# One float32r split for both heads of a pair, and two magnitude buffers, in a fused attention and expert kernel

## The chip, the cores and the metric

The kernel runs on one core of a Trainium2 chip. The metric is the device time of one execution in microseconds, taken as the median of three runs. A profiled execution of the same program gives the rows below.

## The reference, cut to what matters

```python
# q, k, v: (4 batches, 8 heads, 576 positions, 64 per head), float32
scores = (q @ k.T) / 8 + bias              # bias: -slope(head) * |i - j|
attn = softmax(where(0 <= i - j < 128, scores, -1e9))
x = (attn @ v).transpose(0, 2, 1, 3).reshape(2304, 512)
h = x @ w_in                               # (2304, 2048)
g = (a0 + a1*h + a2*h^2 + a3*h^3) / (1 + |b0|*|h| + |b1|*h^2 + 1e-6)
x = g @ w_out                              # w_in, w_out arrive as float64
e = argmax(x @ w_gate); p = softmax(x @ w_gate)[e]
out = p * (relu(x @ w1[e]) @ w2[e])        # 8 experts, 512 -> 1024 -> 512
```

## The kernel before, in words

The 2304 tokens are cut into nine chunks of 256 (`c` from 0 to 8). For each chunk there is an attention step over four pairs of heads (`hp`), which leaves `x` as two float32r halves `xh` and `xl`, and a first feed-forward step over eight pairs of weights (`j` from 0 to 7): `up` makes `h_ps`, `rational` makes `gh` and `gl` from it, and `down` adds to `y_ps` two steps later. While chunk `c` is in its feed-forward step, the attention of chunk `c + 1` runs beside it. Behind the ninth chunk the tokens are sorted by expert and ten chunks of expert work follow, with `load_split` fetching the expert weights.

Float32 accuracy on TensorE comes from splits. A tensor `a` becomes `hi = round(a)` in float32r and `lo = a - hi`, and products are made with both. For q and k of chunks 2 to 8 (`c >= PACK`) the kernel loads q and k of two heads so that each head lies twice over the 128 partitions: 64 rows for the high half and 64 for the low half. For each head `r` of the pair, it then takes one tile `qk` of the pool `rawp` and cuts it into `q2`, `kh` and `kl`. ScalarE (ACT) copies q into `q2` (L279) and k into `kh` (L280), VectorE (DVE) overwrites the lower half of `q2` with the remainder (L281), and GpSimd (POOL) makes `kl` (L284). TensorE (PE) makes the scores of one head by two matmuls (L307), one with `kh`, one with `kl`. Seven chunks of four pairs make 28 pairs, so each of these four lines stands 56 times in the program.

The first 16 weights arrive as float64 and are converted on the chip during chunk 0 (`convert`): `fetch64`, then `magnitude64` (ACT takes the absolute value, L174; DVE clamps it, L175), then `split64` (DVE L186, L189, L192; ACT L195; POOL L196). Weights 0 to 13 use tiles of the pool `ring`. Weights 14 and 15 come in halves: their raw halves share the two buffers of `rawp` with the `qk` tiles, and their magnitudes share the three buffers of the pool `ahp` with `ah` of `rational`. In the expert stage `load_split` takes `ah` and `u` buffers too, for every third weight (L212; its ACT copy is L215, its remainder L216).

`rational` uses `ah` (L387, freed by POOL at L392) and `u`, `qq`, `r0` from the pool `ep`, two buffers each. `u` is written by ACT (L388), worked on by DVE (L395, L396, L399, L405), copied by ACT (L408) and freed by POOL (L409, `gl`). The tiles of one name go round their buffers in the order of the program text, so a new tile waits until the one that had the buffer is freed.

The order on each engine is not written out by hand: the program is recorded, and a scheduler puts the instructions of the five queues in order before launch. Each engine then works its queue strictly in that order.

Of the kernel before, what the change touches and what calls it, by code (L numbers as in the profile page):

```python
# [11 lines left out]
F32 = mybir.dt.float32  # L12
F32R = mybir.dt.float32r
# [4 lines left out]
ALU = mybir.AluOpType  # L18
# [4 lines left out]
P = 128  # L23
T = 256
# [5 lines left out]
PACK = 2  # L30
# [11 lines left out]
def attention_rational_moe_kernel(  # L42
# [11 lines left out]
    nc = tc.nc  # L54
    B, _, S = qT.shape
    H, D, W = 8, 64, 128
    NT, DM = out.shape
# [8 lines left out]
    NSTAT = NCH  # L66

    const = ctx.enter_context(tc.tile_pool(name="const", bufs=1))
    ahp = ctx.enter_context(tc.tile_pool(name="ahp", bufs=3))
    xp = ctx.enter_context(tc.tile_pool(name="xp", bufs=2))  # L70
    rawp = ctx.enter_context(tc.tile_pool(name="rawp", bufs=RAWB))
    ring = ctx.enter_context(tc.tile_pool(name="ring", bufs=RING))
    ep = ctx.enter_context(tc.tile_pool(name="ep", bufs=2))
    ap_ = ctx.enter_context(tc.tile_pool(name="ap", bufs=2))
# [32 lines left out]
        out=upper, in_=ones, pattern=[[1, P]], compare_op=ALU.is_gt, fill=0.0,  # L107
# [11 lines left out]
    for h in range(H):  # L119
        sl = 2.0 ** (-8.0 * (h + 1) / H)  # L120
        nc.vector.tensor_scalar(
            out=bm[:, h, :], in0=rel, scalar1=-sl * D ** 0.5, scalar2=None, op0=ALU.mult
        )
        nc.gpsimd.affine_select(
            out=bm[:, h, :], in_=bm[:, h, :], pattern=[[-1, 2 * W]], compare_op=ALU.is_ge,
# [27 lines left out]
    mags = {}  # L153
# [14 lines left out]
    def magnitude64(f):  # L168
        if f < EARLY:
            mags[f] = [ring.tile([P, 2 * DM], F32, name="mag", tag="ring")]  # L170
        else:
            mags[f] = [ahp.tile([P, DM], F32, name="mag", tag="ah") for _ in range(2)]
        for raw, a in zip(raws[f], mags[f]):
            nc.scalar.activation(out=a, in_=raw.bitcast(F32)[:, :, 1], func=AF.Abs)  # L174
            nc.vector.tensor_scalar(  # L175
                out=a, in0=a, scalar1=F64_LEAST, scalar2=F64_MOST, op0=ALU.max, op1=ALU.min
            )
# [87 lines left out]
    def attention(c, xh, xl):  # L265
        for hp in range(H // 2):
# [5 lines left out]
            tiles, kc = load_qkv(c, hp, q_sb, k_sb, v_sb)  # L272


            qks = []
            for r in range(2 if c >= PACK else 0):
                qk = rawp.tile([P, 2 * DM], F32R, name="qk", tag="raw")
                q2, kh, kl = qk[:, 0:T], qk[:, T:T + kc], qk[:, 2 * T + W:2 * T + W + kc]
                nc.scalar.copy(q2, q_sb[:, r, :])  # L279
                nc.scalar.copy(kh, k_sb[:, r, 0:kc])  # L280
                nc.vector.tensor_tensor(  # L281
                    out=q2[D:P], in0=q_sb[D:P, r, :], in1=q2[D:P].bitcast(F32), op=ALU.subtract
                )
                nc.gpsimd.tensor_tensor(  # L284
                    out=kl, in0=k_sb[:, r, 0:kc], in1=kh.bitcast(F32), op=ALU.subtract
                )
                qks.append((q2, kh, kl))
            x_ps = ps_x.tile([P, T], F32, name="x_ps")
            for L, qcol, k0, wn, bo, blocks in tiles:
                s_ps = [ps_s.tile([P, 2 * W], F32, name="s_ps") for _ in range(2)]  # L290
# [5 lines left out]
                for r in range(2):  # L296
                    if c < PACK:
                        nc.tensor.matmul(
                            s_ps[r][0:L, 0:wn],
                            q_sb[D * r:D * r + D, qcol:qcol + L],  # L300
                            k_sb[D * r:D * r + D, k0:k0 + wn],
                            start=True, stop=True,
                        )
                        continue
                    q2, kh, kl = qks[r]
                    for i, kk in enumerate((kh, kl)):
                        nc.tensor.matmul(  # L307
                            s_ps[r][0:L, 0:wn], q2[:, qcol:qcol + L], kk[:, k0:k0 + wn],
                            start=(i == 0), stop=(i == 1),
                        )  # L310
                for r in range(2):
# [447 lines left out]
```

## Time and profile before

| | |
|---|---|
| median of three runs | 933.65 us (932.35 to 934.86) |
| the profiled execution, its own time | 939.27 us |
| its span, first to last instruction | 937.5 us |
| busy in the span: PE, DVE, ACT, POOL | 846.0, 729.0, 610.9, 486.5 us |
| mean granted TensorE clock | 0.962 of full speed |

The span is what the rows below show; some 1.8 us lie around it. A busy time is a sum over the whole span, and the stages differ: chunk 0 with its conversion, chunks 1 to 8, the sorting, and the experts. A granted clock under 1 means that TensorE ran a part of that stretch at the lower of its two levels, 1.2 GHz instead of 2.4 GHz.

### The profile page before, as it was taken

The page shows a single profiled execution, that of the slowest core. Times are in us where ns is not written, and L with a number is a line of the kernel's source. Part 1 is how long each engine was busy: PE and PEld are TensorE (multiplying, and loading weights), DVE is VectorE, ACT ScalarE, POOL GpSimd, SP SyncE. Part 2 cuts the span into 40 slices and gives each one's busy share as a digit, 9 for nine tenths or more (in the row PEclk, how much of TensorE's full clock was granted, in tenths as well). Part 3 has the DMA queues.
Part 4 walks back from the last instruction along what each step waited for, and adds up shares of the span by engine and source line. Part 5 has one row for each costly group of instructions (what it writes and reads, how often), then busy time and mean ns, then how long its engine had stood idle before and what let it go on. Part 6 is the DMA issues. An engine that isn't in the chain of part 4 may idle for free. (4 is left out here: it accounts for less than half of the span.)

```text
span 937.5 us, 16318 instructions
## 1 busy us (share of the span) xinstructions
PE 846.0 (90%) x5550; PEld 727.4 (78%) x5550; DVE 729.0 (78%) x1428; ACT 610.9 (65%) x1286; POOL 486.5 (52%) x403
## 2 busy tenths in 40 slices
PE   4547789998999899999999999999889999999994
PEld 2325568886888788878878878888778999999993
DVE  7999999797897998898987978869756985555510
ACT  5566658776887687778778768766636755555510
POOL 5444446553564555545645455535547875555500
PEclk9997989999999899999999999999988999999997
DMA  8554021123123222122122221100448976668300
GB/s 317 208 171 135 9 82 38 60 61 87 36 62 96 36 67 68 38 67 67 30 66 64 63 71 33 38 23 3 129 134 309 321 264 225 225 225 266 128 6 19
DMA packets 69959, 101.88 MB, mean 109 GB/s; under 512 B 14705, under 2 KB 47345, under 8 KB 68082
## 3 DMA queue, kind: packets, MB, share of 16 engines
q1 hardware_dynamic: 64658, 86.11, 28.9%
q0 software_dynamic: 5216, 14.70, 4.4%
q8 instruction: 45, 0.74, 0.3%
q14 instruction: 40, 0.33, 0.1%
HBM read 91.13 MB, written 10.17 MB: 108 GB/s over the span
## 5 line engine op out<-in xcount | busy, mean ns | idle before, releaser
L366 PE MATMUL h_ps<-x,w 128*128 128x256 f32 x896 | 261.3, 294 | 14.3 <-ACT w L195 5.2
L367 PE MATMUL h_ps<-x,w 128*128 128x256 f32 x896 | 261.5, 292 | 1.6 <-DVE x L354 1.2
L368 PE MATMUL h_ps<-x,w 128*128 128x256 f32 x896 | 260.8, 291 | 2.4 <-POOL w L196 1.6
L366 PEld LDWEIGHTS h_ps<-x,w 128*128 128x128 f32 x896 | 175.5, 197 | 24.4 <-ACT w L195 6.2
L375 PE MATMUL y_ps<-w,gh 128*128 128x512 f32 x448 | 182.4, 407 | 0.6 <-ACT gh L653 0.3
L367 PEld LDWEIGHTS h_ps<-x,w 128*128 128x128 f32 x896 | 176.5, 197 | 8.1 <-DVE x L354 2.3
L368 PEld LDWEIGHTS h_ps<-x,w 128*128 128x128 f32 x896 | 176.4, 197 | 6.7 <-POOL w L196 2.6
L376 PE MATMUL y_ps<-w,gh 128*128 128x512 f32 x448 | 179.6, 401 | 0.0
L377 PE MATMUL y_ps<-w,gl 128*128 128x512 f32 x448 | 170.7, 402 | 0.1
L409 POOL TENSOR_TENSOR gl<-u,gh 128x512 fp32r<-128x512 f32 x72 | 102.0, 1417 | 104.1 <-ACT gh L408 79.2
L392 POOL TENSOR_TENSOR qq<-qq,ah 128x512 f32<-128x512 f32 x72 | 101.2, 1405 | 96.1 <-ACT qq L389 93.0
L216 POOL TENSOR_TENSOR w<-rawh,w 128x512 fp32r<-128x512 f32 x60 | 86.7, 1467 | 52.8 <-ACT w L215 51.9
L377 PEld LDWEIGHTS y_ps<-w,gl 128*128 128x128 f32 x448 | 86.0, 192 | 19.0 <-issue 1.2
L317 ACT ACTIVATE p_sb<-p_sb,nm 128x256 f32<-128x256 f32 (+4 forms) x160 | 75.0, 470 | 38.3 <-DVE nm L312 37.8
L375 PEld LDWEIGHTS y_ps<-w,gh 128*128 128x128 f32 x448 | 86.4, 193 | 15.8 <-issue 1.5
L376 PEld LDWEIGHTS y_ps<-w,gh 128*128 128x128 f32 x448 | 86.5, 193 | 14.4 <-issue 0.2
L284 POOL TENSOR_TENSOR qk<-k_sb,qk 128x384 fp32r<-128x384 f32 (+1 forms) x56 | 65.5, 1180 | 38.0 <-ACT qk L280 30.7
L399 DVE SCALAR_TENSOR_TENSOR u<-u,co,r 128x512 f32<-128x512 f32 x72 | 64.8, 901 | 13.3 <-ACT r L394 12.8
L196 POOL TENSOR_TENSOR w<-mag,w 128x1024 fp32r<-128x1024 f32 (+1 forms) x18 | 44.8, 2489 | 51.6 <-ACT w L195 51.6
L395 DVE TENSOR_TENSOR u<-u,h_ps 128x512 f32<-128x512 f32 x72 | 48.9, 679 | 28.5 <-ACT u L388 28.3
L408 ACT CAST gh<-u 128x512 fp32r<-128x512 f32 x72 | 44.5, 618 | 38.6 <-DVE u L405 38.5
L216 DVE TENSOR_TENSOR w<-raw,w 128x1024 fp32r<-128x1024 f32 x30 | 49.4, 1646 | 25.7 <-ACT w L215 25.6
(140 smaller groups left out, 1673.9 us busy)
## 6 DMA issues: line engine op xcount, KB each, us to landing
rawh<-epack SPq DMA_DIRECT2D x100, 256.0 KB, 4.9
raw<-epack SPq DMA_DIRECT2D x30, 512.0 KB, 5.6
raw<-wpack SPq DMA_DIRECT2D x14, 1024.0 KB, 6.9
v_sb<-vv SPq DMA_DIRECT2D x92, 64.0 KB, 2.1
k_sb<-kT SPq DMA_DIRECT2D x28, 192.0 KB, 3.4
q_sb<-qT SPq DMA_DIRECT2D x40, 128.0 KB, 2.7
yd<-y_sb POOLq DMA_DIRECT2D x18, 256.0 KB, 2.6
k_sb<-kT SPq DMA_DIRECT2D x16, 160.0 KB, 3.0
```

The source lines that it names most:

```text
L216: (nc.gpsimd if i in POOLLO else nc.vector).tensor_tensor(out=w[:, 1, cs], in0=raw, in1=w[:, 0, cs].bitcast(F32), op=ALU.subtract)
L284: nc.gpsimd.tensor_tensor(out=kl, in0=k_sb[:, r, 0:kc], in1=kh.bitcast(F32), op=ALU.subtract)
L317: nc.scalar.activation(out=p_sb[0:L, r, 0:wn], in_=p_sb[0:L, r, 0:wn], func=AF.Exp, scale=-1.0, bias=nm[0:L, r:r + 1], accum_out=su[0:L, r ...
L366: nc.tensor.matmul(out_ps, w[:, 0, ws], xh[:, k, :], start=(k == 0), stop=False)
L367: nc.tensor.matmul(out_ps, w[:, 0, ws], xl[:, k, :], start=False, stop=False)
L368: nc.tensor.matmul(out_ps, w[:, 1, ws], xh[:, k, :], start=False, stop=(k == KD - 1))
L375: nc.tensor.matmul(y_ps[t], gh[:, i, ts], w[:, 0, DM:], start=a, stop=False)
L376: nc.tensor.matmul(y_ps[t], gh[:, i, ts], w[:, 1, DM:], start=False, stop=False)
L377: nc.tensor.matmul(y_ps[t], gl[:, i, ts], w[:, 0, DM:], start=False, stop=z)
L392: nc.gpsimd.tensor_tensor(out=qq, in0=qq, in1=ah, op=ALU.mult)
L399: nc.vector.scalar_tensor_tensor(out=u, in0=u, scalar=co[:, 0:1], in1=r0, op0=ALU.add, op1=ALU.mult)
L409: nc.gpsimd.tensor_tensor(out=gl, in0=u, in1=gh.bitcast(F32), op=ALU.subtract)
```

## The change

Both heads of a pair are split by one instruction per engine: `q2` is a tile of its own (a single buffer of 2 KB per partition in the pool of the attention), and `kh` and `kl` of both heads each take one of the two buffers of `rawp`. To pay for `q2`, the pool `ahp` goes from three buffers to two, and the magnitudes of weights 14 and 15 take one `ah` and one `u` buffer instead of two `ah`. The matmuls and their number stay the same.

```diff
-    ahp = ctx.enter_context(tc.tile_pool(name="ahp", bufs=3))
+    ahp = ctx.enter_context(tc.tile_pool(name="ahp", bufs=2))
...
-            mags[f] = [ahp.tile([P, DM], F32, name="mag", tag="ah") for _ in range(2)]
+            mags[f] = [
+                pool.tile([P, DM], F32, name="mag", tag=tag) for pool, tag in ((ahp, "ah"), (ep, "u"))
+            ]
...
-            qks = []
-            for r in range(2 if c >= PACK else 0):
-                qk = rawp.tile([P, 2 * DM], F32R, name="qk", tag="raw")
-                q2, kh, kl = qk[:, 0:T], qk[:, T:T + kc], qk[:, 2 * T + W:2 * T + W + kc]
-                nc.scalar.copy(q2, q_sb[:, r, :])
-                nc.scalar.copy(kh, k_sb[:, r, 0:kc])
+            if c >= PACK:
+                q2 = ap_.tile([P, 2, T], F32R, name="q2", bufs=1)
+                kh, kl = (
+                    rawp.tile([P, 2 * DM], F32R, name=name, tag="raw")[:, 0:2 * kc]
+                    .rearrange("p (r k) -> p r k", r=2) for name in ("kh", "kl")
+                )
+                nc.scalar.copy(q2, q_sb)
+                nc.scalar.copy(kh, k_sb[:, :, 0:kc])
                 nc.vector.tensor_tensor(
-                    out=q2[D:P], in0=q_sb[D:P, r, :], in1=q2[D:P].bitcast(F32), op=ALU.subtract
+                    out=q2[D:P], in0=q_sb[D:P], in1=q2[D:P].bitcast(F32), op=ALU.subtract
                 )
                 nc.gpsimd.tensor_tensor(
-                    out=kl, in0=k_sb[:, r, 0:kc], in1=kh.bitcast(F32), op=ALU.subtract
+                    out=kl, in0=k_sb[:, :, 0:kc], in1=kh.bitcast(F32), op=ALU.subtract
                 )
-                qks.append((q2, kh, kl))
...
-                    q2, kh, kl = qks[r]
                     for i, kk in enumerate((kh, kl)):
                         nc.tensor.matmul(
-                            s_ps[r][0:L, 0:wn], q2[:, qcol:qcol + L], kk[:, k0:k0 + wn],
+                            s_ps[r][0:L, 0:wn], q2[:, r, qcol:qcol + L], kk[:, r, k0:k0 + wn],
```

The scheduler makes a new order of it from the conversion of weight 14 on. Two places matter below. The first is POOL's queue at the end of chunk 0. Here `mag_1071` is the second half of weight 15, `qk_1397` and `qk_1402` (before) or `kl_1399` (of the change) belong to the first pair of chunk 2, and `u_990`, `u_1135`, `u_1191` to `rational` for `j` = 4, 5, 6. POOL's rows before:

```order
L284 TENSOR_TENSOR qk_1397<-k_sb_1383,qk_1397 128x384
L409 TENSOR_TENSOR gl_995<-u_990,gh_994 128x512
L392 TENSOR_TENSOR qq_1193<-qq_1193,ah_1192 128x512
L196 TENSOR_TENSOR w_1087<-mag_1071,w_1087 128x512
L284 TENSOR_TENSOR qk_1402<-k_sb_1383,qk_1402 128x384
L409 TENSOR_TENSOR gl_1140<-u_1135,gh_1139 128x512
```

POOL's rows of the change, at the same place:

```order
L411 TENSOR_TENSOR gl_995<-u_990,gh_994 128x512
L394 TENSOR_TENSOR qq_1193<-qq_1193,ah_1192 128x512
L288 TENSOR_TENSOR kl_1399<-k_sb_1383,kh_1398 128x768
L198 TENSOR_TENSOR w_1087<-mag_1071,w_1087 128x512
L411 TENSOR_TENSOR gl_1140<-u_1135,gh_1139 128x512
```

The two remainders of 384 columns, one on either side of the last half weight, have become one of 768 columns ahead of it.

The second place is DVE's queue just before that. `u_905` and `u_990` are those of `j` = 3 and 4, `mag_942` is the second half of weight 14, `mag_1070` the first of weight 15. DVE's rows before:

```order
L192 SCALAR_TENSOR_TENSOR mag_942<-raw64_925,mag_942 128x512
L322 RECIPROCAL ri_1221<-ri_1221 128x2
L312 ISA p_sb_1244,nm_1245<-s_ps_1242,bm_110 128x256
L312 ISA nm_1245 128x1
L312 ISA p_sb_1244,nm_1245<-s_ps_1243,bm_110 128x256
L312 ISA nm_1245 128x1
L175 TENSOR_SCALAR mag_1070<-mag_1070 128x512
L399 SCALAR_TENSOR_TENSOR u_905<-u_905,co_102,r0_908 128x512
L327 TENSOR_TENSOR p_sb_1219<-p_sb_1219,ri_1221 128x512
L354 TENSOR_TENSOR x_513<-x_ps_1017,x_513 128x256
L186 TENSOR_SCALAR mag_1070<-mag_1070 128x512
L405 SCALAR_TENSOR_TENSOR u_905<-qq_907,u_905 128x512
```

DVE's rows of the change from the end of `u_905` on:

```order
L407 SCALAR_TENSOR_TENSOR u_905<-qq_907,u_905 128x512
L323 TENSOR_REDUCE ri_1246<-sum0_188 128x2
L188 TENSOR_SCALAR mag_942<-mag_942 128x512
L324 RECIPROCAL ri_1246<-ri_1246 128x2
L177 TENSOR_SCALAR mag_1070<-mag_1070 128x512
L191 SCALAR_TENSOR_TENSOR mag_942<-raw64_925,mag_942 128x512
L329 TENSOR_TENSOR p_sb_1244<-p_sb_1244,ri_1246 128x512
L404 SCALAR_TENSOR_TENSOR qq_992<-qq_992,qc_106,r0_993 128x512
L188 TENSOR_SCALAR mag_1070<-mag_1070 128x512
L194 SCALAR_TENSOR_TENSOR mag_942<-raw64_925,mag_942 128x512
L285 TENSOR_TENSOR q2_1397<-q_sb_1382,q2_1397 64x512
```

Before, the second half of weight 14 was finished ahead of the end of `u_905`, and weight 15 had begun; in the change four of its DVE steps come behind it. In the rows that follow these in the change stand the steps of `u_990`.

## Rows read from the trace of the kernel before

**Rows 1.** Busy time by stretch of the span, engine by engine, with the granted clock.

```profile
core 0: us, PE busy (x) PEld busy (x) DVE busy (x) ACT busy (x) POOL busy (x), PEclk, DMA share, GB/s
98.00:156.00 58.00, 46.68 (x267) 38.10 (x268) 57.67 (x93) 36.72 (x74) 32.08 (x21) 0.88 0.18 50
156.00:610.00 454.00, 438.41 (x3096) 378.87 (x3095) 390.04 (x915) 348.07 (x818) 238.72 (x192) 0.98 0.21 58
610.00:720.00 110.00, 100.09 (x612) 87.05 (x611) 75.96 (x137) 62.50 (x107) 55.07 (x45) 0.92 0.33 111
720.00:937.00 217.00, 204.65 (x1322) 186.11 (x1320) 112.56 (x118) 102.33 (x165) 113.53 (x83) 0.98 0.56 190
```

**Rows 2.** PE's waits from 156 to 610 us: total us, times, longest.

```profile
PE pt_ps L336 <- DVE p_sb L327: 6.4, 6, 3.2
PE h_ps L366 <- ACT x L353: 1.9, 2, 1.1
PE s_ps L307 <- DVE qk L281: 1.4, 2, 0.8
```

**Rows 3.** L281 and L284 by source line: ns minimum/median/maximum.

```profile
L281 DVE TENSOR_TENSOR qk<-q_sb,qk x56: 416/476/2756, 139.4 to 601.5; 64x256 fp32r<-64x256 f32 x56
...
L284 POOL TENSOR_TENSOR qk<-k_sb,qk x56: 858/1166/2496, 136.2 to 600.4; 128x384 fp32r<-128x384 f32 x48, 128x320 fp32r<-128x320 f32 x8
```

**Rows 4.** Groups by shape, whole span: busy us, mean ns, idle before.

```profile
L281 DVE TENSOR_TENSOR qk<-q_sb,qk 64x256 fp32r<-64x256 f32 x56 | 41.3, 742 | 3.3 <-ACT qk L279 1.8
L327 DVE TENSOR_TENSOR p_sb<-p_sb,ri 128x512 f32<-128x512 f32 x44 | 40.7, 925 | 0.9
...
L284 POOL TENSOR_TENSOR qk<-k_sb,qk 128x384 fp32r<-128x384 f32 x48 | 58.0, 1218 | 26.9 <-ACT qk L280 20.9 <-PE y_ps L377 2.0 <-PE s_ps L307 1.6
L409 POOL TENSOR_TENSOR gl<-u,gh 128x512 fp32r<-128x512 f32 x72 | 102.0, 1417 | 104.1 <-ACT gh L408 79.2 <-issue 24.0 <-POOL qq L392 0.7
L196 POOL TENSOR_TENSOR w<-mag,w 128x1024 fp32r<-128x1024 f32 x14 | 38.6, 2757 | 49.3 <-ACT w L195 49.3
...
L279 ACT CAST qk<-q_sb 128x256 fp32r<-128x256 f32 x56 | 22.4, 402 | 7.0 <-PE s_ps L307 6.5 <-DMA q_sb<-qT 0.4
L280 ACT CAST qk<-k_sb 128x384 fp32r<-128x384 f32 x48 | 24.4, 511 | 1.2 <-DMA k_sb<-kT 1.2
L408 ACT CAST gh<-u 128x512 fp32r<-128x512 f32 x72 | 44.5, 618 | 38.6 <-DVE u L405 38.5
L195 ACT CAST w<-mag 128x1024 fp32r<-128x1024 f32 x14 | 14.6, 1044 | 17.5 <-DVE mag L192 17.2 <-DVE ri L322 0.3
```

**Rows 5.** Timeline of DVE, then of POOL, near 97 us: start, us.

```profile
96.90 2.84 DVE L175 TENSOR_SCALAR mag<-mag 128x1024 f32<-128x1024 f32 x1
...
100.32 0.68 DVE L186 TENSOR_SCALAR mag<-mag 128x1024 int32<-128x1024 int32 x1
...
96.41 2.78 POOL L196 TENSOR_TENSOR w<-mag,w 128x1024 fp32r<-128x1024 f32 x1 [5.58 <-ACT w L195]
```

**Rows 6.** L399 and L396 by source line: ns minimum/median/maximum.

```profile
L399 DVE SCALAR_TENSOR_TENSOR u<-u,co,r x72: 730/748/1792, 95.6 to 672.5; 128x512 f32<-128x512 f32 x72
...
L396 DVE SCALAR_TENSOR_TENSOR u<-u,co,h_ps x72: 720/746/749, 86.9 to 670.5; 128x512 f32<-128x512 f32 x72
```

**Rows 7.** Timeline at the end of chunk 0: `u` written, `gl` made.

```profile
124.66 0.77 ACT L388 ACTIVATE u<-h_ps,co 128x512 f32<-128x512 f32 x1
...
122.75 1.28 POOL L409 TENSOR_TENSOR gl<-u,gh 128x512 fp32r<-128x512 f32 x1 [3.60 <-ACT gh L408]
129.74 1.63 POOL L409 TENSOR_TENSOR gl<-u,gh 128x512 fp32r<-128x512 f32 x1 [2.60 <-issue]
```

**Rows 8.** As the experts begin: timelines of POOL and ACT; DMA issues, KB, us to landing.

```profile
663.75 1.45 POOL L392 TENSOR_TENSOR qq<-qq,ah 128x512 f32<-128x512 f32 x1 [2.12 <-ACT qq L389]
...
670.43 0.63 ACT L215 CAST w<-rawh 128x512 fp32r<-128x512 f32 x1
...
rawh<-epack SPq DMA_DIRECT2D x100, 256.0 KB, 4.9
```

## The prediction

> **What bounds the kernel now.** I read the busy times by stretch first, then what TensorE (PE) waits for in the stretch that the change touches most, and then the price of the split's instructions by shape. The cuts between the stretches are mine: chunk 0's conversion of weights ends near 156 us, attention ends near 610 us, the experts are under way by 720 us.
>
> From 156 to 610 us PE is busy 438.41 of 454 us, and its granted clock is 0.98 [rows 1]. So PE sets the time there. What another engine can give back is the 15.6 us in which PE is idle, and at most 0.02 x 454 = 9 us of clock. DVE comes next with 390 us, ACT has 348 and POOL 239. Of the 28 pairs all but the first are split there: 27 pairs, 54 of the 56 calls of each line. PE's largest named wait is for the normalized probabilities of DVE (L327), 6.4 us in 6 waits; it waits 1.4 us for the split of q (L281) and 1.9 us for `x` [rows 2]. The first is a wait for DVE's queue, the second for the work that is changed.
>
> From 98 to 156 us it is otherwise: DVE is busy 57.67 of 58 us, PE 46.68 [rows 1]. DVE sets the time there, and the magnitudes of weights 14 and 15 are part of its load. Behind 720 us PE is busy 204.65 of 217 us, and no instruction that the change rewrites runs there.
>
> **The change part by part.** PE's work is the same: the same matmuls on operands of the same shape. 0 us.
>
> *The split of q, DVE part (L281).* Two operations of 64x256 become one of 64x512. The trace has none of that shape; the nearest are the 128x512 operations with two operands in SBUF. By means, two cost 2 x 0.742 us and one of 512 columns 0.925 (L327) [rows 4], so a pair saves 0.56 us, and 27 pairs 15 us. By minima, two cost 2 x 0.416 [rows 3] and one 0.730 (L399) [rows 6]: 0.10 us per pair, 2.8 us in all. The means hold waits behind POOL, and one operation waits once where two wait twice; but not each pair waits. I take the middle, 9 us of DVE's 390.
>
> *The split of k, POOL part (L284).* Two operations of 384 columns cost 2 x 1.218 us. One of 768 lies between 1.417 (512 columns, L409) and 2.757 (1024 columns, L196) [rows 4]; halfway is 2.09. That saves 0.35 us per pair, 9 us over 27 pairs. The ends are a saving of 1.02 and a loss of 0.32 us per pair, 28 us and -9 us. I take halfway, since 768 is halfway in columns.
>
> *The copies on ACT.* For q, 2 x 0.402 becomes 0.618 (512 columns, L408); for k, 2 x 0.511 becomes 0.83, halfway between 0.618 and 1.044 (L195) [rows 4]. That is 0.19 us each and 10 us over 27 pairs. ACT is busy 348 of 454 us, so nearly all of this lies beside PE. If that cover were gone, the 10 us would be the price.
>
> *A longer hold of POOL against DVE.* Near 97 us a DVE step of 1024 columns took 2.84 us beside a POOL operation that ran from 96.41 to 99.19 us; another of that size took 0.68 beside none [rows 5]. L399 reads two operands in SBUF and reaches 1.792 us, while L396, which reads PSUM, never exceeds 0.749 [rows 6]. So DVE steps of some kinds wait until a POOL operation has ended. The change makes the longest hold in attention 0.87 us longer (2.09 against 1.218) while the sum of the holds falls by 9 us. PE waited for a step of that kind (L327) in only 6 places of the stretch [rows 2], so 6 x 0.87 = 5 us bounds the loss when each of these is hit in full. I take no loss, since the sum falls.
>
> The Trainium skill (SBUF — State Buffer, the section that sets engine ports apart from DMA ports) says that VectorE and GpSimd hold a shared pair of ports as an exclusive lock for a whole instruction, and that the other is blocked fully. The trace agrees with its 2.84 us against 0.68. By that rule alone a merged instruction is a longer block, which speaks against this change; by the rows the sum of the blocks falls.
>
> *The later start of head 0.* Head 0's scores need the `kl` of both heads now, 0.87 us later than before; head 1's come 0.35 us earlier. PE waited only 1.4 us for such work, and has `up` and `down` matmuls queued in between. 0 us, at most 28 x 0.87 = 24 us if every pair stood on PE's path; the row puts it far nearer to nothing.
>
> *Two `ah` buffers.* `ah` lives from ACT's L387 to POOL's L392, and `u` of the same step, with two buffers before and after, lives longer, to L409. So `u` binds first in the chunks: 0 us. In the expert stage `load_split` loads the half weight in `ah` one step later: it waits for the L392 of 663.75 to 665.20 us. A landing takes 4.9 us, so it is there at 670.1, and its ACT copy ran at 670.43 [rows 8]. The half in `u` is queued behind it on SP and waits for `gl`, as before. 0 us, at most 1.
>
> *The magnitude in `u`.* This is the dear part. The magnitudes of weights 14 and 15 now take turns with `u` of `rational`: `u` of `j` = 4 takes the buffer of `j` = 3, not that of `j` = 2. Before, it was written at 124.66 us, 0.6 us behind the `gl` that freed its buffer, which ended at 124.03. The `gl` of `j` = 3 ended at 131.37 [rows 7], so the bound of this wait is 6.7 us. But the order of DVE in the change ends `u_905` (`j` = 3) ahead of four conversion steps of weight 14, and puts them, with steps of weight 15, between it and `u_990`. Conversion and arithmetic of 512 columns cost 0.7 to 1.8 us a step [rows 6], so four steps bring that `gl` forward by 3 to 7 us and fill DVE meanwhile. DVE has to do the same work to the end of this stretch. 0 us, bounds -1 and +6.7. In POOL's queue the remainder of 768 columns stands ahead of the last half weight, which delays that by 2.09 - 1.22 = 0.9 us at most; it is the half that `down` uses, two steps later.
>
> **The sum.** DVE gets about 9 us lighter and is held off for some 9 us less from 156 to 610 us. PE's 15.6 us of idle time do not vanish with that, because most of it is the order of the queues and not load. I take a fifth, 3.1 us, and 0.4 us of clock. That fifth is a choice: of the 15.6 us, 7.8 are waits for L327 and L281, and I let two fifths of these go. All else is 0. The profiled execution took 939.27 us, 1.8 of it around the span: 939.27 - 3.5 = 935.8. It stands 5.6 us above the median of the runs, so the median comes to 933.65 - 3.5 = 930.2 us.
>
> **The rivals.** About 0.3% (2.8 us) is what a measurement of this kernel can tell from no change.
>
> *Hidden: no change.* The relief lands in DVE's, ACT's and POOL's own idle time. For it: PE is busy 97% and each of the three has at least 64 us of slack. Against it: half of PE's idle time is named as waits for DVE. Time 933 us, within 931 to 936. Chance 0.32.
>
> *A larger gain.* If the waits for DVE and the lower clock both go, PE gets 7.8 us and some 3 us of clock. For it: DVE by means is 15 us lighter. Against it: a new order makes new waits. Time 923 us. Chance 0.12.
>
> *Slower by the magnitude in `u`.* Place: 120 to 156 us. If the scheduler's order does not fill the wait, `u` of `j` = 4 to 6 each starts late. It decides from the point at which the chain from `gl` to the next `gl` outlasts the conversion steps between. For it: DVE has 0.3 us of slack there, and PE at a clock of 0.88 has little work that is ready. Against it: the order shown. Price 6.7 us: 940 us. Chance 0.14.
>
> *Slower by the longer hold.* Five to six us if the six waits for L327 grow by 0.87 and no relief reaches PE: 939 us. Against it stands the falling sum. Chance 0.09. The rule of the skill named above is the one that would bring it.
>
> My own forecast has 0.33, and its own range is 927 to 932.
>
> **How the numbers follow.** Faster than 930.85 us: the forecast's 0.33 and the larger gain's 0.12, so 0.45. Same: 0.32. Slower than 936.45: 0.14 + 0.09 = 0.23. The range reaches from the larger gain, 923, to the magnitude's price, 940, and leaves out a tenth on either side, where several waits come together.
>
> **What would show it.** In the profile after: PE's busy time within 1% of before, 28 operations less on DVE, 28 on POOL and 56 on ACT. The merged DVE step between 0.73 and 0.93 us, POOL's near 2.1, the q copy 0.62, the k copy 0.83. PE idle from the conversion's end to the end of attention near 12 us, with less wait for L327 and the q split. The stretch of chunk 0's end neither longer nor shorter by over 2 us; if it is longer, a wait of DVE or ACT for `gl` in 120 to 150 us stands in its place. The expert stage the same to 1 us. The prediction is wrong if PE's waits sit in new places, as the whole order is new, or if POOL's merged step costs nearer 2.7 us than 2.1.

## The result and the profile after

The change is slower: 945.46 us (median of 4 runs, 944.90 to 946.40) against 933.37 us for the kernel before (4 runs), a ratio of 1.0129 with a 95% interval of 1.0112 to 1.0147. Forecast were 930.2 us and a range of 923 to 940; the time lies 5.5 us above the range. The profiled execution took 945.52 us, at its median, with a span of 943.8 us. That of the kernel before stood 5.9 us above its median, so the two traces show only half of the 12 us between them: 6.3 us of span. These are 8.3 us more in which PE is idle and 2.0 us less in which it is busy (844.0 us, before 846.0), at a mean granted clock of 0.973 (before 0.962).

In the changed file the q copy is L283, the k copy L284, DVE's remainder of q L285 and POOL's remainder of k L288; lines behind them stand two higher than before. Busy time by stretch of the kernel after, which answers to [rows 1]:

```profile
core 0: us, PE busy (x) PEld busy (x) DVE busy (x) ACT busy (x) POOL busy (x), PEclk, DMA share, GB/s
98.00:156.00 58.00, 46.87 (x280) 37.94 (x281) 57.20 (x97) 38.78 (x77) 31.84 (x20) 0.91 0.18 52
156.00:610.00 454.00, 434.45 (x3066) 376.42 (x3066) 384.20 (x871) 334.30 (x749) 226.62 (x162) 0.98 0.21 57
610.00:720.00 110.00, 95.28 (x582) 81.80 (x579) 73.37 (x144) 61.73 (x108) 54.84 (x44) 0.95 0.27 94
```

From 156 to 610 us DVE, ACT and POOL are lighter, as intended, by 6, 14 and 12 us. PE is idle for 454 - 434.45 = 19.6 us instead of 15.6, and runs 30 matmuls fewer in that stretch. From 610 to 720 us it is idle for 14.7 us instead of 9.9. What PE waits for from 156 to 610 us in the kernel after (total us, times, longest), beside [rows 2]:

```profile
PE s_ps L309 <- DVE q L285: 7.5, 3, 4.8
PE h_ps L368 <- DVE u L398: 4.1, 7, 1.0
PE y_ps L377 <- ACT gh L410: 1.7, 2, 1.5
```

The waits for the normalized probabilities, 6.4 us before, are gone from the top. In their place stand the merged remainder of q, 7.5 us in three waits where its two parts cost 1.4 us, and `u`, for which the kernel before has

```profile
PE h_ps L366 <- DVE u L396: 1.2, 3, 0.5
```

The merged remainders by source line of the kernel after (ns minimum/median/maximum), beside [rows 3]:

```profile
L285 DVE TENSOR_TENSOR q<-q_sb,q x28: 689/1562/4374, 130.1 to 600.1; 64x512 fp32r<-64x512 f32 x28
...
L288 POOL TENSOR_TENSOR kl<-k_sb,kh x28: 1540/1849/2630, 142.7 to 600.5; 128x768 fp32r<-128x768 f32 x24, 128x640 fp32r<-128x640 f32 x4
```

The four merged operations as groups by shape (busy us, mean ns, idle before), beside [rows 4]:

```profile
L288 POOL TENSOR_TENSOR kl<-k_sb,kh 128x768 fp32r<-128x768 f32 x24 | 47.7, 1987 | 27.4 <-ACT kh L284 26.4 <-POOL gl L411 0.9
L285 DVE TENSOR_TENSOR q<-q_sb,q 64x512 fp32r<-64x512 f32 x28 | 44.2, 1577 | 7.2 <-ACT q L283 6.5
...
L284 ACT CAST kh<-k_sb 128x768 fp32r<-128x768 f32 x24 | 20.0, 832 | 5.1 <-PE s_ps L309 3.1 <-DMA k_sb<-kT 2.0
...
L283 ACT CAST q<-q_sb 128x512 fp32r<-128x512 f32 x28 | 17.3, 618 | 0.7 <-DMA q_sb<-qT 0.7
```

ACT's and POOL's prices are close to those forecast. DVE's is not: 1.577 us, more than the 2 x 0.742 us that it replaces in the trace before.

**A pair of heads to the next.** PE's idle time has grown by only 4 us from 156 to 610 us, so I followed the split itself. First the kernel before near 247 us, timelines of ACT, DVE, POOL and PE (start, us), as the split of one pair follows the scores of the pair ahead:

```profile
246.55 0.41 ACT L279 CAST qk<-q_sb 128x256 fp32r<-128x256 f32 x1 [0.83 <-PE s_ps L307]
247.37 0.50 ACT L280 CAST qk<-k_sb 128x384 fp32r<-128x384 f32 x1
...
247.60 0.99 DVE L281 TENSOR_TENSOR qk<-q_sb,qk 64x256 fp32r<-64x256 f32 x1
...
248.28 1.20 POOL L284 TENSOR_TENSOR qk<-k_sb,qk 128x384 fp32r<-128x384 f32 x1
...
248.24 0.40 PE L307 MATMUL s_ps<-qk 128*128 128x256 f32 x2
...
250.33 0.40 PE L307 MATMUL s_ps<-qk 128*128 128x256 f32 x2
```

Head 0's buffer comes free before head 1's last score matmuls at 248.24 us. So head 0 is copied at 246.55 us, and its first scores start 1.7 us behind the last of the pair ahead. The same pair in the kernel after:

```profile
245.46 0.82 ACT L284 CAST kh<-k_sb 128x768 fp32r<-128x768 f32 x1
246.19 0.61 ACT L283 CAST q<-q_sb 128x512 fp32r<-128x512 f32 x1
...
249.99 0.69 DVE L285 TENSOR_TENSOR q<-q_sb,q 64x512 fp32r<-64x512 f32 x1
...
246.41 1.85 POOL L288 TENSOR_TENSOR kl<-k_sb,kh 128x768 fp32r<-128x768 f32 x1 [1.22 <-ACT kh L284]
...
243.97 0.28 PE L309 MATMUL s_ps<-kl,q 128*128 128x256 f32 x1
...
252.21 0.28 PE L309 MATMUL s_ps<-kh,q 128*128 128x256 f32 x1
```

The merged copies can't begin until both heads are scored (the last matmul is that of 243.97 us), POOL's step holds until 248.26, DVE comes to the remainder at 249.99, behind other steps of its queue, and the next scores start 8.0 us behind the last. PE doesn't stand still meanwhile: in this place it is busy in all of the 8.0 us, with `up`, `down` and other matmuls. So a longer time without scores is not by itself time lost. Over all 27 steps from a pair to the next, worked out from the starts and ends of these instructions in the two traces, the first copy begins on average 1.1 us ahead of the end of the last score before and 0.7 us behind it after; ahead of it in 19 steps before, in 6 after, and in those 6 by less than 0.1 us (the `kh` buffer is free one matmul before the last). The time without scores between two pairs grows from 7.0 to 9.1 us, and the scores of a pair are squeezed from 10.0 into 8.1 us. From the first scores of one pair to those of the next it takes 17.2 us instead of 17.1, some 4.5 us in all 27 steps.

### The profile page after: what moved, and what is told of

Its sections match the earlier page's. It is cut to its first block, busy times and chain, and to the rows that moved or that the text cites. A ratio compares the mean times of both kernels' runs of the same rounds, so it can differ in the third digit from the quotient of the medians.

```text
span 943.8 us, 16168 instructions
## 1 busy us (share of the span) xinstructions
PE 844.0 (89%) x5550; PEld 725.7 (77%) x5550; DVE 721.4 (76%) x1400; ACT 604.5 (64%) x1230; POOL 478.5 (51%) x375
## 5 line engine op out<-in xcount | busy, mean ns | idle before, releaser
L411 POOL TENSOR_TENSOR gl<-u,gh 128x512 fp32r<-128x512 f32 x72 | 104.1, 1446 | 133.3 <-ACT gh L410 99.9
L288 POOL TENSOR_TENSOR kl<-k_sb,kh 128x768 fp32r<-128x768 f32 (+1 forms) x28 | 54.4, 1943 | 37.7 <-ACT kh L284 36.8
L217 ACT CAST w<-rawh 128x512 fp32r<-128x512 f32 x100 | 57.0, 618 | 17.3 <-PE y_ps L379 10.8
```

The lines of the kernel that those rows point to most:

```text
L217: nc.scalar.copy(w[:, 0, cs], raw)
L288: nc.gpsimd.tensor_tensor(out=kl, in0=k_sb[:, :, 0:kc], in1=kh.bitcast(F32), op=ALU.subtract)
L411: nc.gpsimd.tensor_tensor(out=gl, in0=u, in1=gh.bitcast(F32), op=ALU.subtract)
```

## The experiments

The first theory was the queue theory: DVE's merged remainder stands behind POOL's. Its rivals were the magnitude in `u`, and an order theory (every new order of the queues has waits of its own). Later came the overlap theory: what costs is that head 0's split no longer overlaps with the scores of the pair ahead. Times are medians, ratios are against the kernel before on the same chip. Columns 4 to 6 are worked out from each profiled execution over the 27 steps: start of the first ACT copy less the end of the last score of the pair ahead (us, mean), steps in which it came first, and time without scores (us, mean). The expectations quote that last figure as 6.8 us for the kernel before, where the first pair was counted as a zero.

| kernel | us | ratio, 95% interval | copy less last score | copy first | no scores |
|---|---|---|---|---|---|
| before | 933 to 937 | 1 | -1.1 | 19 | 7.0 |
| the change | 945.46 | 1.0129 (1.0112 to 1.0147) | 0.7 | 6 | 9.1 |
| mags_alone | 937.48 | 1.0023 (1.0007 to 1.0039) | -1.5 | 20 | 6.6 |
| k_merged | 960.55 | 1.0286 (1.0253 to 1.0320) | 0.9 | 6 | 9.2 |
| q_first | 944.31 | 1.0094 (1.0066 to 1.0123) | 0.7 | 0 | 8.4 |
| before_k_first | 943.10 | 1.0085 (1.0057 to 1.0112) | -0.5 | 14 | 7.8 |
| heads_in_pair_order | 950.77 | 1.0152 (1.0124 to 1.0181) | -0.5 | 15 | 9.3 |
| pair_in_heads_order | 974.91 | 1.0418 (1.0391 to 1.0445) | 0.3 | 13 | 7.8 |
| q_merged | 941.03 | 1.0062 (1.0042 to 1.0081) | -0.7 | 15 | 9.3 |
| copies_merged | 953.10 | 1.0182 (1.0156 to 1.0208) | 1.0 | 5 | 9.1 |
| before_kload_first | 937.91 | 1.0023 (1.0008 to 1.0039) | -0.6 | 18 | 7.3 |
| after_kload_first | 955.12 | 1.0210 (1.0190 to 1.0231) | 0.8 | 8 | 9.0 |
| before_kh_both_first | 939.46 | 1.0046 (1.0029 to 1.0063) | -1.0 | 19 | 7.2 |
| after_kh_both_first | 944.15 | 1.0092 (1.0075 to 1.0109) | 0.8 | 9 | 8.9 |
| before_waits_for_both | 950.67 | 1.0164 (1.0135 to 1.0192) | 0.8 | 0 | 8.2 |
| heads_in_pair_buffers | 942.18 | 1.0087 (1.0056 to 1.0119) | 1.1 | 4 | 8.6 |
| before_three_raw | 959.24 | 1.0261 (1.0229 to 1.0293) | -9.3 | 27 | 8.4 |
| after_three_raw | 972.73 | 1.0413 (1.0383 to 1.0442) | -6.9 | 25 | 9.5 |
| one_copy_per_head | 948.15 | 1.0137 (1.0097 to 1.0178) | -0.4 | 12 | 7.9 |
| two_gl_buffers | 936.19 | 1.0008 (0.9989 to 1.0026) | -1.3 | 19 | 6.5 |

### The parts of the change

**mags_alone** has the change's magnitude buffers and the split per head.

```
-    ahp = ctx.enter_context(tc.tile_pool(name="ahp", bufs=3))
+    ahp = ctx.enter_context(tc.tile_pool(name="ahp", bufs=2))
...
-            mags[f] = [ahp.tile([P, DM], F32, name="mag", tag="ah") for _ in range(2)]
+            mags[f] = [
+                pool.tile([P, DM], F32, name="mag", tag=tag) for pool, tag in ((ahp, "ah"), (ep, "u"))
+            ]
```

> Only the magnitude part: two ah buffers, and the magnitudes of weights 14 and 15 in one ah and one u buffer; the splits per head as before. Queue theory (the loss comes from the merged split: the merged q remainder on DVE stands behind the merged k remainder on POOL, and PE waits for it): no change, 931 to 936 us. Magnitude theory (the loss is u being shared with the magnitudes, or the third ah buffer): 940 to 946 us, with waits of ACT for gl between 100 and 156 us. Order theory (no step is to blame, each new order of the queues has waits of its own): anywhere from 928 to 946 us, with PE's waits in places that nothing of the change touches.

937.48 us, 0.2% over the kernel before: below the magnitude theory's 940 us, which falls, and 1.5 us above the queue theory's range.

**k_merged** merges k on ACT and POOL and leaves q per head, in the tails of the same raw buffers.

```
+                nc.scalar.copy(kh, k_sb[:, :, 0:kc])
...
+                nc.gpsimd.tensor_tensor(
+                    out=kl, in0=k_sb[:, :, 0:kc], in1=kh.bitcast(F32), op=ALU.subtract
+                )
```

> Only k is split for both heads at once (one ACT copy, one POOL remainder of 768 columns); q stays at one copy and one DVE remainder per head, in the free columns of the kh and kl buffers; three ah buffers and the magnitudes as before. Queue theory: the POOL remainder takes 1.99 us as in the changed kernel and the q remainders that follow it wait, mean of one above the 0.742 us of before; slower than before, but by less than the whole change: 935 to 942 us. Magnitude theory: no change, 931 to 936 us. Order theory: 928 to 946 us.

960.55 us, worse than the change and above the range of every theory. The remainders of k_merged as groups by shape (busy us, mean ns, idle before):

```profile
L286 POOL TENSOR_TENSOR kl<-k_sb,kh 128x768 fp32r<-128x768 f32 x24 | 47.3, 1970 | 42.6 <-ACT kh L281 26.8 <-PE pt_ps L336 7.9 <-DVE nm L312 7.1
L283 DVE TENSOR_TENSOR kh<-q_sb,kh 64x256 fp32r<-64x256 f32 x28 | 32.3, 1154 | 1.0
L283 DVE TENSOR_TENSOR kl<-q_sb,kl 64x256 fp32r<-64x256 f32 x28 | 27.5, 983 | 1.3 <-ACT kl L280 0.8
```

DVE's per-head remainders, unchanged in shape, take 1.154 and 0.983 us beside the merged POOL step instead of 0.742. That is the queue theory's mark, on a kernel 2.9% slower; two such waits of 0.2 to 0.4 us a pair are only a part of that.

**q_first** is the change with q copied ahead of k on ACT, so that DVE's remainder is ready before POOL's starts.

```
-                nc.scalar.copy(q2, q_sb)
-                nc.scalar.copy(kh, k_sb[:, :, 0:kc])
+                qi = nc.scalar.copy(q2, q_sb)
+                with tc.issue_after(qi.ins):
+                    nc.scalar.copy(kh, k_sb[:, :, 0:kc])
```

> The changed kernel, with ACT held to the copy of q ahead of the copy of k of each pair (it issued k first for most). All else as in the change. Queue theory: the q remainder starts before POOL's k remainder can, its mean falls from 1.577 us to 0.7 to 1.0, PE's waits for it fall from 7.5 us to under 1.5 us, and the time falls by 4 to 9 us to 936 to 941 us. Magnitude theory: 943 to 947 us, as the change. Order theory: the mean of the remainder falls too, but the time may lie anywhere from 930 to 948 us.

The remainders of q_first, as groups by shape:

```profile
L289 POOL TENSOR_TENSOR kl<-k_sb,kh 128x768 fp32r<-128x768 f32 x24 | 48.5, 2019 | 44.0 <-ACT kh L285 43.7
L286 DVE TENSOR_TENSOR q<-q_sb,q 64x512 fp32r<-64x512 f32 x28 | 30.5, 1088 | 1.0
```

DVE's step falls from 1.577 to 1.088 us, 13.7 us of DVE time in these steps come back, and PE's wait for them falls from 7.5 to 3.1 us (the queue theory had under 1.5). The time is 944.31 us, above that theory's 936 to 941: the ratio is 1.0094 where the change has 1.0129, a quarter of the loss at the middle, with intervals that overlap. So the queue theory names a real wait, but most of the loss stays when that wait is more than halved.

**q_merged** and **copies_merged** merge other parts: q alone on both its engines, or both ACT copies with the remainders per head.

```
+                q2 = ap_.tile([P, 2, T], F32R, name="q2", bufs=1)
+                nc.scalar.copy(q2, q_sb)
...
+            for r in range(2 if c >= PACK else 0):
+                qk = rawp.tile([P, 2 * DM], F32R, name="qk", tag="raw")
...
+                nc.scalar.copy(kh, k_sb[:, r, 0:kc])
```

> Only q is split for both heads at once (one ACT copy, one DVE remainder); k stays per head, so POOL's remainders are the short ones of 1.2 us. The queue theory: the DVE remainder takes 0.75 to 1.0 us as nothing long stands on POOL beside it, and the time is 934 to 939 us. The order theory gives no sign ahead: 933 to 947 us by what order comes out; a time of 942 or more with a short DVE remainder would speak for it.

```
+                for r in range(2):
+                    nc.vector.tensor_tensor(
+                        out=q2[D:P, r], in0=q_sb[D:P, r], in1=q2[D:P, r].bitcast(F32),
+                        op=ALU.subtract,
+                    )
...
```

> The change with its two ACT copies for both heads, but both remainders per head as before (DVE 64x256 and POOL 128x384, two each). The queue theory: the per-head remainders are again near 0.75 to 0.9 us on DVE and 1.1 to 1.25 us on POOL, and the time is 935 to 940 us. The order theory: the copies still come later for head 0 and the order of the rest is new again, 940 to 947 us.

q_merged took 941.03 us. A row of it, beside the POOL steps of 1.216 us:

```profile
L281 DVE TENSOR_TENSOR q<-q_sb,q 64x512 fp32r<-64x512 f32 x28 | 27.8, 994 | 3.5 <-ACT q L280 2.8
```

0.994 us is within the queue theory's forecast, and the time is 2 us above it, but under the 942 us that would have spoken for the order theory. copies_merged took 953.10 us with no merged remainder at all, above what either theory gave, and its DVE step missed the queue theory's 0.75 to 0.9 us:

```profile
L286 DVE TENSOR_TENSOR q<-q_sb,q 64x256 fp32r<-64x256 f32 x56 | 60.8, 1124 | 8.7 <-ACT q L283 8.2
```

### Order and instructions apart

**before_k_first** is the kernel before with each head's k copied ahead of its q. It does the same work.

```
-                nc.scalar.copy(q2, q_sb[:, r, :])
-                nc.scalar.copy(kh, k_sb[:, r, 0:kc])
+                ki = nc.scalar.copy(kh, k_sb[:, r, 0:kc])
+                with tc.issue_after(ki.ins):
+                    nc.scalar.copy(q2, q_sb[:, r, :])
```

> The kernel before, with ACT held to the copy of k ahead of the copy of q for each head. Nothing else. Queue theory: the q remainder of 64x256 now comes behind POOL's k remainder, its mean rises from 0.742 us to 1.1 to 1.4, PE waits for it more than the 2.4 us of before, and the time rises by 2 to 8 us to 935 to 941 us. Magnitude theory: no change, 931 to 936 us. Order theory: 928 to 946 us.

943.10 us, 0.85% more, with nothing merged. The remainder stayed at 0.779 us, where the queue theory had 1.1 to 1.4: the time rose without the wait that was to raise it.

**heads_in_pair_order** and **pair_in_heads_order** impose the recorded issue order of the one kernel on the instructions of the other, by edges that order without a wait:

```
+    for _names in json.loads(zlib.decompress(base64.b64decode(_ORDER))):
+        _names = [n for n in _names if f"I-{n}" in _traced]
+        for _a, _b in zip(_names, _names[1:]):
+            tc.add_manual_dep(
+                _traced[f"I-{_b}"], f"I-{_a}",
+                mybir.DependencyInfo(mybir.DependencyClass.NoSync, mybir.DependencyReason.DATA),
+                reason="order",
+            )
```

> The split is made per head as before (two instructions each, magnitudes in ah and u as in mags_alone), but every instruction that this kernel shares with the change is issued on its engine in the order that it has in the change; the split's own instructions are left where the scheduler puts them. Nothing of the reference is left out. The queue theory (the merged remainders' long holds cost the time): about 937 us, as mags_alone, at most 940, since every remainder is short again. The order theory (the new order of everything else costs it): 942 to 947 us, as the change, with the loss again between 300 and 610 us.

> The change itself, its split made for both heads by one instruction each, but on PE, ACT, POOL and SP every instruction that it shares with mags_alone is issued in mags_alone's order; on DVE the order is left to the scheduler, since mags_alone's own order there can't be kept when both heads need the second raw buffer at once. The queue theory: 944 us or more, as the change, the DVE remainder still near 1.5 us in the middle. The order theory: 935 to 940 us, near mags_alone. Between the two (941 to 943) both would hold a share.

Per-head instructions in the change's order took 950.77 us, above the ranges of both theories and no faster than the change itself (945.46; the intervals of the ratios overlap). So the loss is there without merged instructions. That they cost nothing in that order isn't shown: this kernel loses time at chunk 0's end that the change doesn't (PE busy 42.93 us from 98 to 156 us, 46.87 in the change), and the split's own instructions stand in new places. Its remainder of q per head, with that of mags_alone:

```profile
L283 DVE TENSOR_TENSOR qk<-q_sb,qk 64x256 fp32r<-64x256 f32 x56 | 53.0, 956 | 2.9 <-ACT qk L281 1.4
...
L283 DVE TENSOR_TENSOR qk<-q_sb,qk 64x256 fp32r<-64x256 f32 x56 | 46.8, 841 | 3.3 <-ACT qk L281 1.8
```

Two of these take 1.91 us, and 1.68 us in mags_alone, both more than the 1.577 us of the merged one. The 0.742 us was the price in one order only. The largest waits of PE from 156 to 610 us in heads_in_pair_order:

```profile
PE pt_ps L338 <- DVE p_sb L329: 7.1, 8, 2.9
PE h_ps L368 <- DVE u L398: 6.1, 4, 4.0
```

The wait for `u` that the change shows (4.1 us; 1.2 us in the kernel before) is here without any merged step. The other way round came out at 974.91 us, 35 us above the order theory's 935 to 940; the queue theory's "944 us or more, as the change" has it only by its first half. My reading, which no run shows apart, is that an order that scores head 0 while head 1 is still to be split can't be kept cheaply by instructions that need both. It tells that the merge fits another order than the one before, and no more.

**The same perturbation on both kernels.** In the kload kernels a pair's k is loaded ahead of its q, in the kh kernels the score matmuls are traced as kh of both heads, then kl of both.

```
-            for dst, at, src, s0, s1 in ((q_sb, col, qT, s, s + n), (k_sb, kc, kT, w0, s + n)):
+            for dst, at, src, s0, s1 in ((k_sb, kc, kT, w0, s + n), (q_sb, col, qT, s, s + n)):
```

> The kernel before with one line turned round: a pair's k is loaded ahead of its q, so SP issues the same transfers in another order and the scheduler makes another order of the rest. No work is added or taken. The order theory: another order has other waits, 936 to 945 us. The theory that the merged instructions themselves cost the change its 12 us: 933 to 937 us, since nothing is merged here.

> The change with the same line turned round. The theory that the merged instructions themselves cost the time: 10 to 13 us above before_kload_first, as the change stands above the kernel before. The order theory: its distance to before_kload_first differs by 5 us or more from those 12, either way; a distance under 4 us would say that the merge itself costs little.

```
+                for i, r in ((0, 0), (0, 1), (1, 0), (1, 1)):
```

> The kernel before with the four score matmuls of a tile traced as kh of head 0, kh of head 1, kl of head 0, kl of head 1, the same matmuls in another order. The order theory: 936 to 945 us. The theory that the merged instructions cost the time: 933 to 937 us.

> The change with its score matmuls traced in that same order: both heads' kh first, so that the merged kl is wanted two matmuls later. The theory that the merged instructions cost the time by POOL's long remainder: 938 to 942 us, a part of the loss back, and 4 to 8 us above before_kh_both_first. The order theory: anywhere in 936 to 948 us, its distance to before_kh_both_first not that of the change to the kernel before.

The distances of the change's kind to its partner are 945.46 - 933.37 = 12.1, 955.12 - 937.91 = 17.2 and 944.15 - 939.46 = 4.7 us. They scatter by more than 5 us, as the order theory has it, but all have one sign, which chance would give in one case of four. The rows of the table that keep the first copy ahead in 18 to 20 steps lie at 933 to 940 us. That gave the overlap theory.

### The overlap

**before_waits_for_both** merges nothing. It adds one wait: head 0 is copied only behind the last score matmul of the pair ahead.

```
+                    if r == 0 and scored:
+                        tc.add_manual_dep(
+                            copied.ins, scored[-1].ins.name,
+                            mybir.DependencyInfo(
+                                mybir.DependencyClass.Sync, mybir.DependencyReason.DATA
+                            ),
+                            reason="both heads scored",
+                        )
```

> The kernel before, with one wait added: a pair's head 0 is copied only when the last score matmul of the pair before it is done, as the change's copies for both heads must wait; everything else is made per head as before. The overlap theory (the change lost what before had: head 0's split runs while head 1 of the pair before is still being scored): the mean time from a pair's last score to the next pair's first grows from 6.8 us to 7.8 us or more, and the time is 941 to 947 us. The theory that the merged instructions cost by their length: 936 to 939 us.

950.67 us, 1.64% over the kernel before (1.35 to 1.92%), and 8.2 us without scores: more than the change lost and than the theory forecast, with nothing merged. It is nearly twice what the dearest of the other orders of unchanged work cost (0.85%). So taking the overlap away, with the order that the scheduler makes around the wait, is enough for a loss of this size. It doesn't leave everything else as it was: PE's wait for the remainder of q grows from 1.4 to 4.9 us, and the remainder's mean from 0.742 to 0.978 us.

**heads_in_pair_buffers** has the change's buffers and four operations per head.

```
-                nc.scalar.copy(q2, q_sb)
-                nc.scalar.copy(kh, k_sb[:, :, 0:kc])
...
+                for r in range(2):
+                    nc.scalar.copy(q2[:, r], q_sb[:, r, :])
+                    nc.scalar.copy(kh[:, r], k_sb[:, r, 0:kc])
...
```

> The change's buffers (one q2 for both heads, kh and kl each in a raw buffer for both heads), but all four operations per head as before. The overlap theory: the buffers come free only when both heads are scored, so 941 to 950 us, although every instruction is as short as before. The theory that the merged instructions cost by their length: 936 to 940 us.

942.18 us, 0.87% over (0.56 to 1.19%), as the overlap theory forecast. So two thirds of the change's loss appear with its buffers and nothing merged, the 0.23% of the magnitudes among them. This isn't clear of the order theory: before_k_first cost 0.85% by order alone. Nor do the parts add up: with the same buffers and merged copies copies_merged cost 1.82%, and with merged remainders as well, the change, 1.29%.

**one_copy_per_head** loads a head's q and k into one tile and copies them at once, 56 ACT instructions fewer as in the change, but within a head.

```
-                nc.scalar.copy(q2, q_sb[:, r, :])
-                nc.scalar.copy(kh, k_sb[:, r, 0:kc])
+                nc.scalar.copy(qk[:, 0:T + kc], qk_all[:, r, 0:T + kc])
```

> Per head as before, but a head's q and k are loaded into one tile and copied by one ACT instruction of 640 columns instead of two: ACT is relieved by about as many instructions as in the change (56 fewer), and head 0's split still needs nothing of head 1. The overlap theory: head 0's copy still starts ahead of the last score of the pair before it in more than half of the pairs, the time from there to the next first score stays below 7.5 us, and the time is 932 to 940 us; the copy near 0.72 us in place of 0.40 and 0.51. The order theory: any order may come out, up to 945 us, whatever the overlap.

948.15 us: the forecast of the overlap theory was wrong, and so was its premise, since the copy came first in only 12 steps and the time without scores was 7.9 us. The copy as a group by shape, with what it waited for:

```profile
L279 ACT CAST qk<-qk_sb 128x640 fp32r<-128x640 f32 x48 | 33.8, 724 | 17.3 <-PE s_ps L306 10.5 <-DMA qk_sb<-kT 6.7
```

It now waits for both loads, 6.7 us for the later one, and q and k share one tile. This agrees with the theory after the fact and doesn't test it.

**before_three_raw** and **after_three_raw** give overlap back with a third raw buffer, paid for with a `gl` buffer, in the change with a `gh` buffer too. **two_gl_buffers** is the control of the first: mags_alone with the `gl` buffer given up and no third raw buffer.

```
-RAWB = 2
+RAWB = 3
...
-        gl = ep.tile([P, 2, T], F32R, name="gl", bufs=3)
+        gl = ep.tile([P, 2, T], F32R, name="gl", bufs=2)
```

> mags_alone with a third raw buffer, paid for with one of three gl buffers, so that head 0 of the next pair can be split a head earlier. The overlap theory: the time between the pairs' scores falls below 6.3 us and the time is 930 to 937 us; if the lost gl buffer costs, up to 940. The theory of the merged instructions says nothing here but no change from mags_alone, 936 to 939 us.

> The change with a third raw buffer (paid for with one of three gh and one of three gl buffers), so that the next pair's merged k copy need not wait for the last score of the pair before it; q2 stays single. The overlap theory: the k copy starts before that last score and a part of the loss comes back, 936 to 942 us, if the two lost buffers cost nothing. The theory that the merged instructions cost by their length: 944 us or more.

> The control of before_three_raw: mags_alone with two gl buffers in place of three and the two raw buffers as they were. If the lost gl buffer is what cost before_three_raw its time, this takes 950 to 960 us or more, and the third raw buffer gave nothing or a little. If the third raw buffer cost the time by a split that runs too early, this takes 937 to 942 us, and the overlap theory in its simple form (the earlier the split, the better) falls.

The control took 936.19 us, no worse than mags_alone, so the lost `gl` buffer is free. The third raw buffer cost before_three_raw 23 us where the overlap theory had a gain, although the first copy came on average 9.3 us ahead of the last score. In the simple form, the earlier the better, the overlap theory falls. ACT's largest waits of before_three_raw from 156 to 610 us, and with them DVE's largest:

```profile
ACT qk L281 <- DMA q_sb<-qT: 30.2, 14, 5.7
...
DVE qk L283 <- ACT qk L281: 20.1, 14, 2.6
```

In two_gl_buffers the same copy waits 0.4 us for the load; its largest wait, and DVE's line:

```profile
ACT qk L281 <- PE s_ps L309: 6.9, 8, 2.0
...
DVE qk L283 <- ACT qk L281: 1.7, 3, 0.6
```

With a buffer free the copy stands so early in ACT's queue that it waits for the load of q, whose tile is single, and holds up 30.2 us of ACT and 20.1 us of DVE behind it. after_three_raw (972.73 us, far above its forecast of 936 to 942) has no control of its own and is left as inconclusive.

## Why the prediction was wrong

- **PE 0 us, ACT's copies, POOL's remainder:** right. 844.0 us of busy PE, 0.618 and 0.832 us for the copies as forecast, 1.987 us against 2.09; DVE has 28 operations fewer, POOL 28, ACT 56.
- **The magnitude in `u`, two `ah` buffers:** near 0, as forecast. mags_alone adds 0.2%, and the stretch from 98 to 156 us is as busy as before. As the experts begin, PE's wait for ACT's copy of a half weight (L215, L217 after) grows from 1.5 to 3.0 us in mags_alone and to 4.0 us in the change, more than the 1 us that was allowed. From the 1,920th of the up matmuls to the 2,688th both traces take 186 us, so the rest of the expert stage is the same.
- **DVE's remainder of q, 0.925 us where 2 x 0.742 stood:** the first step that failed. It took 1.577 us, 0.09 us more than the two, so the relief on DVE did not come from the split (its group went from 41.3 to 44.2 us). DVE got 7.6 us lighter over the span all the same, by other steps: those of L399 went from 64.8 to 60.0 us. "One operation waits once where two wait twice" was wrong in its weight: a step that is ready behind POOL's 1.99 us waits for most of it. The rule of the Trainium skill that was weighed there, the exclusive lock that blocks DVE fully (SBUF — State Buffer, two separate sides), would have pointed to this; the trace agrees with it by 0.689 us at least and 1.562 us at the median. It is not what most of the 12 us are made of, as q_first shows, and per head the remainder costs as much in other orders.
- **The later start of head 0, 0 us:** the step that cost the forecast its sign, as far as the runs tell. It priced the 0.87 us by which `kl` comes later against 1.4 us of wait that PE showed. What it left out is when the merged copies can begin: their buffers are free only when both heads are scored, where head 0's were free before. PE's short wait of before was no sign that PE is indifferent to it: with the overlap taken away and nothing merged, that wait is 4.9 us, in the change 7.5 us. Forcing that wait costs 1.64%, the change's buffers 0.87%.
- **A fifth of PE's idle time, 3.1 us of gain:** it supposed that the order of everything else stays as good as it was. PE's idle time from 156 to 610 us went from 15.6 up to 19.6 us instead of down to near 12, with its waits in new places, which the prediction named as a sign of being wrong. "A new order makes new waits" stood only against the larger gain. The same work in three other orders cost 0.23, 0.46 and 0.85%, so an order alone can outweigh the relief that was forecast.
- **The rivals:** the one that came out slower by the longer hold had a price of 5 to 6 us and a chance of 0.09. Its place, DVE behind POOL, was partly right; its waits (for the probabilities) were not the ones that grew.

What stays open is the cause of each microsecond. Kernels that lost the overlap lie between 942 and 961 us, and neither the time without scores nor DVE's remainder ranks them: q_merged has 9.3 us without scores at 941 us, copies_merged 9.1 us at 953. What follows the times closely is PE's idle time over the whole span (span less busy PE): 91 to 95 us in the kernels up to 942 us, 97 to 102 from 943 to 951, 103 to 111 from 953 to 961. How the change's 12 us divide between the lost overlap and the order that the scheduler then made could not be told apart, because each kernel with another constraint gets another order. A version that beats the kernel before was not found.

## What to carry to other kernels

Before two operations of a pair are merged, ask when their inputs and their buffers come free, not only what the instructions cost: the merged one starts with the later of the two, and what ran between them is lost. A short wait in a profile can be short because of the very overlap that the change removes. Where a scheduler orders the queues, run the unchanged work in a few other orders first: here they spread by 0.9%, and a gain below that, summed from durations, can't be relied on. And read what PE does in a gap before calling it a loss: the longer time between scores was filled with other matmuls in the place shown.

## What the runs showed of the hardware

- One DVE shape has very different prices in kernels of nearly the same work: the 64x256 remainder has a mean of 0.742 us in the kernel before, 0.841 in mags_alone and 1.124 in copies_merged, all beside POOL steps of 1.1 to 1.2 us, and the 64x512 one 0.689 us at least, 0.994 us beside POOL steps of 1.2 us (q_merged), and beside those of 2.0 us 1.088 us where q is copied first (q_first) and 1.577 us where k is in 25 of 28 pairs (the change).
- POOL's 768 columns cost 1.987 us against 1.218 for 384 [rows 4]: 1.63 times for twice the columns. ACT's 640 columns cost 0.724 us and 768 cost 0.832.
- A buffer more made a kernel 23 us slower (before_three_raw against two_gl_buffers). With it the copy stands earlier in a queue that keeps its order, and its waits there for its load grow from 0.4 to 30.2 us.
